# First pair's hash rows ahead of its low halves, over three queues, with the planner's numbers set anew, in a one-core LSH attention and spatial-gating kernel

## The chip, the cores and the metric

The kernel runs on one core of a Trainium2 chip. The metric is the device time of one execution in microseconds (us). The engines are called PE (TensorE, matrix products), DVE (VectorE), ACT (ScalarE), POOL (GpSimd) and SP (SyncE, which here only issues DMAs).

## The reference, cut to what matters

```python
# B, H, S, D = 4, 8, 768, 64; proj is 64 x 6
q_bits = (einsum('bhsd,dk->bhsk', q, proj) > 0)        # six hash bits per query; k_bits alike
mask = q_bucket[:, :, :, None] == k_bucket[:, :, None, :]
scores = where(mask, (q @ k.T) / sqrt(D), -1e9)
attn = softmax(scores)
x = (attn @ v), heads side by side                      # 4 x 768 x 512
h = maximum(x @ w_in, 0); u, vv = halves of h           # 512 columns each
v_n = (vv - mean) / sqrt(var + 1e-6)
v_s = einsum('ts,bsd->btd', w_spatial, v_n) + b_spatial
out = (u * v_s) @ w_out
```

## The kernel before, in words

**Tiles.** The 32 heads are taken as 16 pairs (`p` 0 to 15, four pairs to a batch element); the two heads of a pair lie in the two halves of the partitions. The 768 rows of a pair are worked in six steps (`i` 0 to 5) of 128 rows, so there are 96 score steps, written p.i here (0.0 is the very first, 5.0 the first of pair 5). f32 operands are split in a high and a low f16 half, so that a product is three products of halves.

**One step.** `scores` forms, for both heads, twelve products of halves (tile `hl`) and then four products of hash rows (tile `hk`) in the same PSUM banks: the hash rows push the scores of other buckets far down. For a head worked by queries, DVE then reduces the step to row maxima and moves it to SBUF (`low`, L525, tile `ex`), ACT or POOL forms the bias (`nb`), ACT the exponential (L535) and the f16 high half (L539, tile `pp`), DVE or POOL the low half (`rest`, L543), SP turns it with a DMA (L547, tile `pt`), and `weighted` (L653, `pv`) multiplies by v some steps later. Heads 2, 4, 6 and 8 (one in each of the pairs 1 to 4) are worked by keys: their maxima are formed ahead by `row_max` (tile `mx`), six steps of them before the pair's own first score step. The pairs after that carry only queries.

**Before a pair's first step** its q and k are loaded (`load_qk`), split (`split_qk`: one ACT copy, L412, then two DVE subtractions, L416) and hashed (`hash_rows`): a PE product (`hp`, L371), two small DVE operations (bits, L378, and scale, L382, tile `sg`), and eight DMAs (twelve from pair 5 on) that put the hash rows into `hk` (L393). For pair 0 SP and ACT issue these DMAs, four each; for all others POOL issues them.

**Weights.** Meanwhile 36 pieces of the three weight matrices come in by SP (`fetch`, L293). Those of w_in and w_out are worked by ACT and DVE with one ACT operation (`first`, L309), four DVE operations (L313, L314, L316, L318), an ACT copy (L323) and a DVE subtraction (L328); those of w_spatial only with the last two.

**MLP.** When all four pairs of a batch element are done, its gating MLP becomes filler for PE: six v units, eight u units, eight s units, six o units, cut in chunks of three products (L750) of which there are 128 to a batch element. 24 of them are v chunks and 32 are u chunks. An s unit needs the normalized v of all six v units; its low half is formed by POOL (L892, tile `vn`).

**The order** is not found on the chip. Every operation is recorded with a rank, an estimated duration and what it comes after; a planner in the kernel (`timetable`) plays the engines against these estimates, takes on a free engine the operation of the lowest rank among those that could start (or could within `LOOK`), and gives each a start. The program is then written out in the order of these starts, and on the chip each engine runs its own list strictly in that order. `LATER` shifts ranks by the name of the operation; `LAG0` is by how many steps `weighted` comes behind the scores for heads of the first batch element; the `T_` numbers say how far apart the score steps are in the plan, `begin` being the earliest start of a step. Where the planner sees PE idle for over `GAP`, it puts in small products whose result nobody reads, to keep PE busy (`warm`, L217): 444 of them.

## Time and profile before

| what | value |
|---|---|
| three timed runs | 658.12, 659.49, 662.9 us, median 659.49 |
| profiled execution, its own time | 655.07 us |
| its span in the trace | 653.3 us |
| granted PE clock | 1.00 of full speed throughout |
| busy share of the span | PE 94%, DVE 72%, ACT 73%, POOL 49% |
| instructions | 17683 |

A row of the timeline gives start, duration, engine, line, operation and tiles; "x4" means four instructions merged, and what stands in brackets is the idle time ahead of it and what ended it. An engine name with a q (SPq) is that engine's queue of DMA issues. A row of the stretches gives, after the bounds and the length, the busy time and the number of instructions of each engine. PE busy includes the `warm` products.

### The profile page before, as it was taken

What the parts mean: (1) busy time and instruction counts of PE and PEld (TensorE: products, weight loads), DVE (VectorE), ACT (ScalarE), POOL (GpSimd) and SP (SyncE); (2) the same over time, 40 slices, a digit from 0 to 9 for tenths busy, and PEclk for the clock granted to TensorE, in tenths of its full rate; (3) what the DMA queues carried; (4) which work ended last, traced back from release to release, by engine and by line L of the source; (5) the groups of instructions that cost most, each with busy time, mean ns of one, the idle gap of its engine ahead of it and who ended that gap; (6) DMA issues with size and microseconds to landing.
All of it is one profiled execution on the core that took longest, in us unless ns stands there. A gap on an engine that the chain in (4) does not pass through costs nothing.

```text
span 653.3 us, 17683 instructions
## 1 busy us (share of the span) xinstructions
PE 615.5 (94%) x7076; PEld 374.4 (57%) x7076; DVE 471.1 (72%) x986; ACT 473.7 (73%) x800; POOL 321.8 (49%) x397
## 2 busy tenths in 40 slices
PE   5789999899999999899999999998999999999997
PEld 3466767577555656455555556564555665556553
DVE  6899999898788766758879677765667587365250
ACT  3868776868898977887879887876889967463121
POOL 4565451534686859494638559376749412000000
PEclk9999999999999999999999999999999999999999
DMA  5899988997899999999998999997997989210102
GB/s 186 197 190 227 199 163 174 222 214 145 178 209 188 169 219 198 204 209 198 212 207 147 201 225 148 227 213 138 210 214 130 153 150 158 50 49 0 49 1 96
DMA packets 311682, 108.94 MB, mean 167 GB/s; under 512 B 298144, under 2 KB 301744, under 8 KB 311600
## 3 DMA queue, kind: packets, MB, share of 16 engines
q1 hardware_dynamic: 306256, 106.26, 84.4%
q0 software_dynamic: 5248, 1.52, 1.2%
q8 instruction: 55, 0.90, 0.6%
q14 instruction: 27, 0.22, 0.1%
q10 hardware_dynamic: 96, 0.04, 0.0%
HBM read 27.94 MB, written 6.29 MB: 52 GB/s over the span
## 4 chain that ended last, share of the span: by engine, by line
PE 51%; DVE 15%; DMA 11%; ACT 9%; issue 7%; POOL 5%; SPq 1%; DVEq 0%; POOLq 0%; ACTq 0%
PE sps L750 12%; PE sp L496 9%; PE ops L750 9%; PE pv L653 8%; DMA pt<-pp 6%; PE ups L750 5%; DVE ex L525 4%; PE vps L750 3%; ACT pp L539 3%; ACT ex L535 2%; POOL pp L543 2%; DVE pp L543 2%; PE vpp L750 2%; DMA hk<-sg 2%; DVE mx L600 1%
## 5 line engine op out<-in xcount | busy, mean ns | idle before, releaser
L525 DVE TENSOR_SCALAR_CACHE_REDUCE ex<-sp 128x768 f32<-128x768 f32 x168 | 155.6, 951 | 55.1 <-PE sp L496 53.0
L543 POOL TENSOR_TENSOR pp<-ex,pp 128x768 f16<-128x768 f32 x86 | 140.9, 1646 | 74.2 <-ACT pp L539 53.0
L535 ACT ACTIVATE ex<-ex,nb 128x768 f32<-128x768 f32 x168 | 155.3, 932 | 10.5 <-POOL nb L530 7.3
L539 ACT CAST pp<-ex 128x768 f16<-128x768 f32 x168 | 137.3, 826 | 4.9 <-DMA pt<-pp 3.6
L653 PEld LDWEIGHTS <-pt 128*128 128x128 f16 x3024 | 107.4, 97 | 37.3 <-DMA pt<-pp 13.3
L653 PE MATMUL pv<-vp,pt 128*128 128x65 f16 x3024 | 118.6, 193 | 7.9 <-DMA pt<-pp 7.7
L496 PE MATMUL sp<-hl 64*128 64x384 f16 x1080 | 107.4, 324 | 5.0 <-DVE ex L525 4.7
L393 POOL DMA_DIRECT2D hk<-sg x156 | 79.8, 518 | 50.8 <-issue 15.9
L543 DVE TENSOR_TENSOR pp<-ex,pp 128x768 f16<-128x768 f32 x82 | 79.7, 980 | 34.2 <-ACT pp L539 33.9
L750 PE MATMUL sps<-ws,vn 128*128 128x384 f16 x576 | 100.8, 326 | 0.1
L496 PEld LDWEIGHTS <-hl 64*128 64x128 f16 x1116 | 51.1, 94 | 56.8 <-issue 27.5
L750 PEld LDWEIGHTS <-vn 128*128 128x128 f16 x576 | 53.7, 98 | 33.5 <-issue 0.9
L750 PE MATMUL ops<-wo,g 128*128 128x512 f16 x288 | 66.1, 379 | 1.0 <-DVE sg L378 1.0
L532 ACT ACTIVATE nb<-mr 128x1 f32<-128x1 f32 x123 | 24.1, 197 | 55.9 <-DVE ex L525 55.6
L750 PE MATMUL ups<-xt,wi 128*128 128x384 f16 x348 | 62.8, 326 | 1.2 <-ACT u L919 1.2
L750 PE MATMUL vps<-wi,xt 128*128 128x512 f16 x234 | 56.9, 379 | 1.7 <-DVE sg L378 0.9
L750 PEld LDWEIGHTS <-wi 128*128 128x128 f16 x384 | 35.1, 98 | 24.1 <-issue 3.7
L750 PEld LDWEIGHTS <-g 128*128 128x128 f16 x288 | 26.7, 98 | 31.7 <-issue 1.6
L750 PEld LDWEIGHTS <-xt 128*128 128x128 f16 x288 | 25.5, 97 | 29.5 <-issue 5.4
L496 PE MATMUL sp<-hk 12*128 12x384 f16 (+2 forms) x360 | 37.1, 329 | 4.5 <-DMA hk<-mt 3.5
L940 DVE SCALAR_TENSOR_TENSOR sy<-sps,bt 128x384 f32<-128x384 f32 x32 | 17.8, 555 | 31.0 <-PE sps L750 31.0
L948 ACT CAST g<-sy 128x384 f16<-128x384 f32 x32 | 16.2, 506 | 32.3 <-DVE sy L952 28.8
(112 smaller groups left out, 786.7 us busy)
## 6 DMA issues: line engine op xcount, KB each, us to landing
qk<-kq SPq DMA_DIRECT2D x16, 768.0 KB
out<-o SPq DMA_DIRECT2D x24, 256.0 KB
v<-v SPq DMA_DIRECT2D x12, 384.0 KB
pt<-pp SPq DMA_TRANSPOSE x168
hk<-sg POOLq DMA_DIRECT2D x156, 9.0 KB, 4.0
raw<-w_in SPq DMA_DIRECT2D x8, 256.0 KB
raws<-w_in SPq DMA_DIRECT2D x8, 256.0 KB
vf<-v SPq DMA_DIRECT2D x4, 384.0 KB
```

What stands on the lines that cost most here:

```text
L393: eng.dma_start(out=hkt(p)[D * e + at:D * e + at + 2 * NB, 1 - j // 2, (j % 2) * HS:(j % 2 + 1) * HS], in_=sg[1][32 * j + 16 * e:32 * j + ...
L496: nc.tensor.matmul(ps[e][:, c - halves[0]], lhsT=src[r, l, rows], rhs=src[r, m, cs], start=(a == 0), stop=(a == len(passes) - 1))
L525: nc.vector.tensor_scalar(ex, st["sc", p, i][e], -float(2 ** 28), None, op0=ALU.max, op1=ALU.max, accum_out=st["mx", n][:, i:i + 1])
L532: nc.scalar.activation(nb, mx, AF.Copy, scale=-ISQ)
L535: nc.scalar.activation(st["e32", n, i], st["e32", n, i], AF.Exp, bias=st["nb", n][:, i:i + 1], scale=ISQ)
L539: nc.scalar.copy(st["pp", n, i][:, 0], st["e32", n, i])
L543: eng.tensor_tensor(out=st["pp", n, i][:, 1], in0=st.pop(("e32", n, i)), in1=st["pp", n, i][:, 0], op=ALU.subtract)
L600: nc.vector.reduce_max(st["mx", 2 * p + e][:, i, c:c + 1], ps[e], axis=AX.XY)
L653: nc.tensor.matmul(o, lhsT=l, rhs=m, start=(i == 0 and k == 0), stop=(i == NT - 1 and k == len(todo_) - 1))
L750: nc.tensor.matmul(c[0], lhsT=l(), rhs=r(), start=(j == 0), stop=(j == len(products) - 1))
L940: nc.vector.scalar_tensor_tensor(out=y[0], in0=c[0], scalar=1.0 / (SN * SW), in1=bt[:, hs], op0=ALU.mult, op1=ALU.add)
L948: nc.scalar.copy(gt[h][0][:, d], y[0])
```

## The change

The two small DVE operations and the eight DMAs of pair 0's hash rows get a rank ahead of everything else (`soon`), so that they go before the low halves of the same pair where they can. The eight DMAs are spread: SP issues four, ACT two, POOL two. The load of the third pair is planned behind the first score step. Beside that the planner's numbers change: `relu` later by 0.3, `LAG0` 4 for 3, `T_LAST` 5.8 for 5.95, `LOOK` 0 for 0.05, and products of the rank -9 get no added lateness.

```diff
-    LATER = {'relu': 0.1, 'first': -0.5, ...
+    LATER = {'relu': 0.4, 'first': -0.5, ...
-    def op(e, d, fn, *after, on=(), rank=4, land=0.0, dma=0.0, need=None, gives=None, alone=False):
+    def op(e, d, fn, *after, on=(), rank=4, land=0.0, dma=0.0, need=None, gives=None, alone=False, soon=False):
         later = LATER.get(fn.__name__.strip("<>"), 0.0)
-        if not isinstance(rank, tuple):
+        if soon:
+            rank = (-9, rank[1])
+        elif not isinstance(rank, tuple):
             rank = rank + later
...
-                late = (LATE_D if o.dma else LATE) if a.e == "P" and not (isinstance(a.rank, tuple) and a.rank[1] == 0) else 0.0
+                late = (LATE_D if o.dma else LATE) if a.e == "P" and not (isinstance(a.rank, tuple) and (a.rank[1] == 0 or a.rank[0] == -9)) else 0.0
...
-        t = op("V", 0.54, bits, t, on=[g0], rank=(urgent(p), 2), gives="m")
-        t = op("V", 0.24, scale, t, on=[g0, g1], rank=(urgent(p), 2), alone=True)
+        t = op("V", 0.54, bits, t, on=[g0], rank=(urgent(p), 2), gives="m", soon=p == 0)
+        t = op("V", 0.24, scale, t, on=[g0, g1], rank=(urgent(p), 2), alone=True, soon=p == 0)
...
-                q, eng = HQ_FIRST[e] if p == 0 else HQ_REST
+                q, eng = HQ_FIRST[2 * j + e] if p == 0 else HQ_REST
...
-    LAG, LAG0, LAGK = 4, 3, 2
-    T_FIRST, T_KEYS, T_QUERIES, T_THIRD, T_LAST = 5.0, 5.4, 5.55, 5.75, 5.95
+    LAG, LAG0, LAGK = 4, 4, 2
+    T_FIRST, T_KEYS, T_QUERIES, T_THIRD, T_LAST = 5.0, 5.4, 5.55, 5.75, 5.8
-    LOOK = 0.05
+    LOOK = 0
-    HQ_FIRST = (("S", nc.sync), ("A", nc.scalar))
+    HQ_FIRST = [("SAG"[k], (nc.sync, nc.scalar, nc.gpsimd)[k]) for k in (2, 0, 1, 2, 0, 1, 0, 0)]
...
             if g == 0:
                 hash_rows(1)
                 split_qk(1)
-                load_qk(2)
+                load_qk(2, now)
```

The planner's numbers move instructions on every engine over the whole program. In the changed program all line numbers behind `op` are higher by two. Three places follow.

The first is the start of DVE's list, from behind its first fills to the first two reductions of scores. Before:

```order
L416 SCALAR_TENSOR_TENSOR hl_114<-qk_108,hl_114 128x768 x2
L378 TENSOR_SCALAR sg_0_168<-hp_118,hc 128x384
L435 SCALAR_TENSOR_TENSOR vp_92<-v_0_110,vp_92 128x12x64
L382 TENSOR_SCALAR sg_0_174<-sg_0_168,hc 128x384
L416 SCALAR_TENSOR_TENSOR ws_79<-qk_112,ws_79 128x768 x2
L378 TENSOR_SCALAR sg_1_230<-hp_182,hc 128x384
L382 TENSOR_SCALAR sg_1_233<-sg_1_230,hc 128x384
L525 TENSOR_SCALAR ex_0_295,mr_293<-sp_0_0_241 128x768
L313 TENSOR_SCALAR w_291<-w_291 128x256
L525 TENSOR_SCALAR ex_0_305,mr_303<-sp_0_1_242 128x768
```

And in the changed program:

```order
L380 TENSOR_SCALAR sg_0_193<-hp_114,hc 128x384
L418 SCALAR_TENSOR_TENSOR hl_119<-qk_108,hl_119 128x768
L384 TENSOR_SCALAR sg_0_197<-sg_0_193,hc 128x384
L418 SCALAR_TENSOR_TENSOR hl_119<-qk_108,hl_119 128x768
L437 SCALAR_TENSOR_TENSOR vp_92<-v_0_110,vp_92 128x12x64
L418 SCALAR_TENSOR_TENSOR ws_79<-qk_112,ws_79 128x768 x2
L380 TENSOR_SCALAR sg_1_217<-hp_211,hc 128x384
L384 TENSOR_SCALAR sg_1_237<-sg_1_217,hc 128x384
L527 TENSOR_SCALAR ex_0_270,mr_268<-sp_0_0_219 128x768
L527 TENSOR_SCALAR ex_0_278,mr_276<-sp_0_1_220 128x768
```

Pair 0's bits now come first, its scale stands between the two low halves, and no weight operation stands between the two reductions. On ACT two of pair 0's hash DMAs now stand ahead of the split of pair 1 (tile `ws`), where four stood behind it; ACT's first weight operation, which stood ahead of the first bias, has moved behind the second exponential. On PE, 71 `warm` products stand between the hash products of pair 0 and pair 1 and none between the latter and the first scores, where it was 43 and 39. POOL issues the eight hash DMAs of pair 1 behind its two of pair 0.

The second place is DVE's list around the first step of pair 5 (`ex_0`); `w` and `wo` are weight pieces of w_out. Before:

```order
L525 TENSOR_SCALAR ex_4_2877,mr_2517<-sp_4_1_2786 128x768
L313 TENSOR_SCALAR w_2874<-w_2874 128x256
L328 SCALAR_TENSOR_TENSOR wo_104<-w_2810,wo_103 128x256
L314 TENSOR_SCALAR w_2874<-w_2874 128x256
L316 SCALAR_TENSOR_TENSOR w_2874<-raws,w_2874 128x256
L318 SCALAR_TENSOR_TENSOR w_2874<-raws,w_2874 128x256
L525 TENSOR_SCALAR ex_5_2915,mr_2517<-sp_5_1_2889 128x768
L328 SCALAR_TENSOR_TENSOR wo_104<-w_2874,wo_103 128x256
L525 TENSOR_SCALAR ex_0_2957,mr_2955<-sp_0_0_2924 128x768
L525 TENSOR_SCALAR ex_0_2964,mr_2962<-sp_0_1_2925 128x768
```

And in the changed program:

```order
L527 TENSOR_SCALAR ex_5_2864,mr_2534<-sp_5_1_2820 128x768
L316 TENSOR_SCALAR w_2840<-w_2840 128x256
L330 SCALAR_TENSOR_TENSOR wo_104<-w_2787,wo_103 128x256
L318 SCALAR_TENSOR_TENSOR w_2840<-raw_2703,w_2840 128x256
L527 TENSOR_SCALAR ex_0_2915,mr_2913<-sp_0_0_2879 128x768
L841 BN_STATS bs_0_2921<-vr_0_2902 128x6
L842 BN_AGGR mv_0_2920<-bs_0_2921 128x2
L527 TENSOR_SCALAR ex_0_2947,mr_2945<-sp_0_1_2880 128x768
L320 SCALAR_TENSOR_TENSOR w_2840<-raw_2703,w_2840 128x256
L315 TENSOR_SCALAR w_2917<-w_2917 128x256
```

The last weight operation stood just ahead of pair 5's first reduction and now four pieces of w_out are still being worked when that reduction comes. In DVE's list ahead of it there are 3 fewer of each of L313, L314 and L316, 4 fewer of L318, 4 fewer of L328 and one fewer of L543.

The third place is POOL's list around the last three low halves of the first batch element's normalized v (`vn_1`), in pairs 6 and 7; `hk_81` are pair 7's hash DMAs. Before:

```order
L892 TENSOR_TENSOR vn_1_3356<-vr_3_3345,vn_0_3355 128x512
L543 TENSOR_TENSOR pp_2_3784<-ex_2_3751,pp_2_3784 128x768
L543 TENSOR_TENSOR pp_2_3849<-ex_2_3763,pp_2_3849 128x768
L695 TENSOR_TENSOR xs_3847<-x_3776,xs_3847 128x6x64
L695 TENSOR_TENSOR xs_3847<-x_3778,xs_3847 128x6x64
L393 DMA hk_81<-sg_7_3949 12x384 x12
L892 TENSOR_TENSOR vn_1_3356<-vr_4_3443,vn_0_3355 128x512
L892 TENSOR_TENSOR vn_1_3356<-vr_5_3534,vn_0_3355 128x512
```

And in the changed program:

```order
L894 TENSOR_TENSOR vn_1_3292<-vr_3_3199,vn_0_3291 128x512
L532 TENSOR_SCALAR nb_3574<-mr_3573 128x1
L395 DMA hk_81<-sg_7_3911 12x384 x5
L545 TENSOR_TENSOR pp_3_3976<-ex_3_3918,pp_3_3976 128x768
L545 TENSOR_TENSOR pp_3_4037<-ex_3_3940,pp_3_4037 128x768
L395 DMA hk_81<-sg_7_3911 12x384 x7
L894 TENSOR_TENSOR vn_1_3292<-vr_4_3301,vn_0_3291 128x512
L545 TENSOR_TENSOR pp_5_4158<-ex_5_4132,pp_5_4158 128x768
L545 TENSOR_TENSOR pp_5_4160<-ex_5_4138,pp_5_4160 128x768
L894 TENSOR_TENSOR vn_1_3292<-vr_5_3358,vn_0_3291 128x512
```

Two low halves of scores now stand between the last two. In the plan's order the last `vn_1` stood ahead of step 7.0 and now stands behind it, while on PE the 56th chunk (the last of the v and u units) followed step 6.5 and now follows step 6.3. Over the program there are 481 `warm` products for 444: 71 for 82 ahead of step 0.0, 107 for 92 in pair 0, 141 for 163 in pairs 1 to 4, 99 for 25 in pairs 5 to 7 (89 of them between 6.4 and 7.0) and 63 for 82 after that. The MLP chunks ahead of 5.0 are 4 for 3, ahead of 6.0 they are 37 for 24, ahead of 8.0 they are 80 for 84.

More of the change, by code (lines that the diff above doesn't have):

```diff
@@ L78, in lsh_attention_spatial_gating @@
     TURN = 1.92
-    LATER = {'relu': 0.1, 'first': -0.5, 'bias': -0.3, 'bits': 0.1, 'stats': 0.3, 'half': -0.4, 'copy': 0.6, 'scale': 0.3, 'newton': -0.4, 'low': 0.6, 'exp': -0.1, 'factor': -0.3, 'turn': -0.6, 'rest': -0.1}
+    LATER = {'relu': 0.4, 'first': -0.5, 'bias': -0.3, 'bits': 0.1, 'stats': 0.3, 'half': -0.4, 'copy': 0.6, 'scale': 0.3, 'newton': -0.4, 'low': 0.6, 'exp': -0.1, 'factor': -0.3, 'turn': -0.6, 'rest': -0.1}
     ops = []
@@ L382, in scale @@
             nc.vector.tensor_scalar(sg[1], sg[0], hv[:, 1:2], None, op0=ALU.mult)
-        t = op("P", 0.8, go, at["qk", p], *after, on=[qk], rank=(urgent(p), 3), need=("m", 1))
-        t = op("V", 0.54, bits, t, on=[g0], rank=(urgent(p), 2), gives="m")
-        t = op("V", 0.24, scale, t, on=[g0, g1], rank=(urgent(p), 2), alone=True)
+        t = op("P", 0.8, go, at["qk", p], *after, on=[qk], rank=(urgent(p), 3), need=("m", 1), soon=p == 0)
+        t = op("V", 0.54, bits, t, on=[g0], rank=(urgent(p), 2), gives="m", soon=p == 0)
+        t = op("V", 0.24, scale, t, on=[g0, g1], rank=(urgent(p), 2), alone=True, soon=p == 0)
         at["hk", p] = []
@@ L395, in move @@
                         in_=sg[1][32 * j + 16 * e:32 * j + 16 * e + 2 * NB, :])
-                at["hk", p].append(op(q, 0.53 if q == "G" else 0.75, move, t, on=[g1, k], rank=(urgent(p), 3), land=2.8 if q == "G" else 1.8))
+                at["hk", p].append(op(q, 0.53 if q == "G" else 0.75, move, t, on=[g1, k], rank=(urgent(p), 3), land=2.8 if q == "G" else 1.8, soon=p == 0))
                 if four(p) and j < 2:
```

## The prediction

> **What bounds the kernel now.** I begin with the page's totals.
>
> ```profile
> PE 615.5 (94%) x7076; PEld 374.4 (57%) x7076; DVE 471.1 (72%) x986; ACT 473.7 (73%) x800; POOL 321.8 (49%) x397
> ```
>
> PE is the engine to look at, but 94% is flattered: its busy time includes the `warm` products. So I cut the span where the first scores of pairs 0, 1 and 5 start (13.2, 47.2 and 168.6 us) and at three later step starts, and ask for the busy time of each stretch, then for that of the `warm` line (L217) alone.
>
> ```profile
> 13.20:47.20 34.00, 26.59 (x386) 17.47 (x385) 27.23 (x64) 23.16 (x40) 21.43 (x27) 1.00 0.92 183
> 47.20:168.60 121.40, 112.39 (x1372) 82.19 (x1371) 113.55 (x271) 90.91 (x167) 53.62 (x70) 1.00 0.92 198
> 168.60:270.00 101.40, 95.90 (x1223) 56.07 (x1222) 75.67 (x154) 87.81 (x147) 72.74 (x83) 1.00 1.07 187
> 270.00:411.90 141.90, 140.54 (x1733) 81.13 (x1734) 106.51 (x202) 117.57 (x192) 89.31 (x109) 1.00 1.07 195
> 411.90:548.00 136.10, 131.50 (x1606) 76.21 (x1607) 94.34 (x191) 108.95 (x180) 79.60 (x93) 1.00 0.98 179
> 548.00:653.30 105.30, 100.83 (x670) 55.73 (x669) 43.56 (x91) 40.32 (x74) 1.33 (x3) 1.00 0.18 48
> ```
>
> The columns behind the length are PE, PEld, DVE, ACT, POOL, then the granted clock, the DMA share and GB/s.
>
> ```profile
> 47.20:168.60 121.40, 10.13 (x164) 9.35 (x163) 1.00 0.92 198
> 168.60:270.00 101.40, 1.56 (x25) 1.41 (x25) 1.00 1.07 187
> ...
> sum 653.30, PE 28.89 PEld 26.25; mean PE 4.13 PEld 3.75
> ```
>
> So PE does 615.5 - 28.9 = 586.6 us of real work, which the change leaves as it is. The rest, 653.3 - 586.6 = 66.7 us, is idle time or filler, and only there can the time change. Most of it lies early: nearly all of the first 13.2 us, ahead of the first scores, then 34.0 - 26.59 = 7.4 us idle in pair 0, then 9.0 idle and 10.1 of filler in pairs 1 to 4. From 168.6 us on, MLP chunks fill PE, and 15.9 us of idle time are left in 484.7 us. The early stretch is held by DVE: it is busy 113.55 of 121.40 us there, and waits little for anyone.
>
> ```profile
> DVE ex L525 <- PE sp L496: 2.4, 2, 1.8
> ```
>
> This is DVE's longest wait between 47.2 and 168.6 us: total, times, longest.
>
> **The change part by part: the head.** The first 24 us, by the timeline:
>
> ```profile
> 5.43 1.50 PE L371 MATMUL hp<-qk,hc 128*32 128x384 f32 x8 [5.43 <-DMA qk<-kq]
> 6.84 1.83 DVE L416 SCALAR_TENSOR_TENSOR hl<-qk,hl 128x768 f16<-128x768 f32 x2 [0.77 <-ACT hl L412]
> 6.87 3.24 PE L217 MATMUL warm<-ident 128*128 128x128 f16 x43
> 8.45 1.48 ACT L412 ACTIVATE ws<-qk 128x1536 f16<-128x1536 f32 x1 [0.91 <-DMA qk<-kq]
> 8.58 0.61 DVE L378 TENSOR_SCALAR sg<-hp,hc 128x384 f16<-128x384 f32 x1
> 9.97 0.32 DVE L382 TENSOR_SCALAR sg<-sg,hc 128x384 f16<-128x384 f16 x1
> 10.17 0.85 PE L371 MATMUL hp<-qk,hc 128*32 128x384 f32 x8
> 10.32 4.00 SPq L393 DMA_DIRECT2D hk<-sg  x4
> 10.32 4.00 ACTq L393 DMA_DIRECT2D hk<-sg  x4
> 13.21 4.34 POOL L393 DMA_DIRECT2D ws<-sg  x8 [8.73 <-DVE sg L382]
> 15.37 1.22 PE L496 MATMUL sp<-hk 63*128 63x384 f16 x4 [0.98 <-DMA hk<-sg]
> 16.26 0.96 DVE L525 TENSOR_SCALAR_CACHE_REDUCE ex<-sp 128x768 f32<-128x768 f32 x1 [3.35 <-PE sp L496]
> 18.27 0.43 ACT L309 ACTIVATE w<-raw 128x256 f32<-128x256 f32 x1 [8.33 <-DMA raw<-w_in]
> 18.94 0.95 DVE L525 TENSOR_SCALAR_CACHE_REDUCE ex<-sp 128x768 f32<-128x768 f32 x1
> 19.95 1.13 PE L496 MATMUL sp<-hl 64*128 64x384 f16 x11 [1.54 <-DVE ex L525]
> 23.57 0.48 PE L496 MATMUL mx<-ws 64*128 64x384 f16 x2 [0.95 <-DVE mx L600]
> ...
> DMA to landing us min/median/max: 2.1/4.2/5.5
> ```
>
> Before, scale ends at 10.29 and the hash rows let PE go on at 15.37, 5.1 us later. Now bits start when the hash products end (6.93), then one low half (1.83 / 2) and scale: 6.93 + 0.61 + 0.92 + 0.32 = 8.8. With the same 5.1 us the rows are there at 13.9. PE itself is ready about then: 71 fillers at 3.24 / 43 = 75 ns end at 6.87 + 5.35 = 12.2, the second hash products at 13.1, twelve products at 14.2, the four with the hash rows (1.22 with their wait before; 0.6 unhindered) at 14.8, against 16.6. DVE gains a little less. ACT now issues two DMAs (4.00 / 4 each) ahead of the split of pair 1: 8.8 + 2.0 + 1.48 = 12.3, DVE's two low halves to 14.1, the second bits and scale to 15.0. The first reduction starts at 15.0 for 16.26 and the second at 16.0 for 18.94, because ACT no longer waits until 18.27 for a weight piece ahead of the bias and DVE has no weight operation between the two. The second scores can start at 17.0 for 19.95: 3 us.
>
> What is late next are pair 1's eight hash rows: POOL starts them at 15.0 for 13.21, its last issue stands at 18.8, and with the median 4.2 us to landing they are there at 23.0. The first `row_max` with hash rows needs them, stood at 23.57, and step 0.2 is queued behind it on PE. That gives back most of the 3 us for PE, though exponentials and transposes of steps 0.0 and 0.1 stay ahead. I take **-2 us**, between 0 and -3.
>
> A rule speaks against the third queue. The Trainium skill, "DMA: Bandwidth & Descriptors", section "Issuing engines are not separate DMA queues", says that DMAs of all issuing engines run on the same 16 DMA engines, and that using several saves only the issue time, usually small beside the transfer. The trace half disagrees: issue took 4.00 us and the wait behind it 0.98. By the rule the head would bring 0 for -2. My sum takes nothing from the third queue either, since SP still issues four; it goes by the earlier scale.
>
> **Pairs 1 to 4.** DVE's list ahead of pair 5's first reduction is shorter by 17 weight operations and one low half of scores.
>
> ```profile
> L543 DVE TENSOR_TENSOR pp<-ex,pp 128x768 f16<-128x768 f32 x82 | 79.7, 980 | 34.2 <-ACT pp L539 33.9
> L313 DVE TENSOR_SCALAR w<-w 128x256 f32<-128x256 f32 x24 | 8.6, 363 | 1.5 <-ACT w L309 1.5
> L314 DVE TENSOR_SCALAR w<-w 128x256 uint32<-128x256 uint32 x24 | 7.3, 309 | 0.0
> L318 DVE SCALAR_TENSOR_TENSOR w<-raws,w 128x256 uint32<-128x256 uint32 x12 | 5.6, 465 | 0.0
> L328 DVE SCALAR_TENSOR_TENSOR wo<-w,wo 128x256 f16<-128x256 f32 x8 | 4.4, 554 | 0.7 <-ACT wo L323 0.7
> ```
>
> By the means, L316 taken as L318: 3 x 0.363 + 3 x 0.309 + 7 x 0.465 + 4 x 0.554 + 0.98 = 8.5 us. A stretch in which DVE is 94% busy could shorten by all of that. The other bound is PE: 112.39 us busy there, with 141 fillers for 163 (22 x 0.062 = 1.4 us less), so 111 us are its floor and -10 us the end on that side. At the other end is 0: PE also waits for hash rows and maxima that come by DMA, and in-order lists pass on half of what one engine gains. I take **-5 us**, between 0 and -10. The weight operations come later, in pair 5, where DVE has room (75.67 of 101.40 us).
>
> **Pairs 5 to 7.** Here the change spends its filler too early. By step 6.0, 37 chunks are done for 24, and all 56 chunks of the v and u units are gone after step 6.3. The next ones, of the s units, need all six normalized v, whose low halves POOL forms.
>
> ```profile
> 195.98 1.17 POOL L892 TENSOR_TENSOR vn<-vr,vn 128x512 f16<-128x512 f32 x1
> 230.34 2.28 POOL L892 TENSOR_TENSOR vn<-vr,vn 128x512 f16<-128x512 f32 x2
> 232.33 0.65 PE L750 MATMUL sps<-ws,vn 128*128 128x384 f16 x3
> ```
>
> Even before, the s units began just as the last low half ended (230.34 + 2.28 = 232.62). Now the last one stands behind step 7.0 and the chunks run out three steps earlier; the plan puts 89 fillers there. At 1.56 / 25 = 62 ns each, the 99 - 25 = 74 more fillers of these pairs cost 4.6 us of PE. I take **+4.6**. It is 0 where they stand in idle time that was there before (5.5 us in this stretch), and +9 if three steps without chunks each leave another 1.5 us open.
>
> **After that** there are 63 fillers for 82: 19 x 0.065 (28.89 / 444) = **-1.2 us**, and the idle time of 1.4, 4.6 and 4.5 us in the last three stretches may move by some 3 us either way (-4 to +3). `T_LAST` moves only starts in the plan; on the chip it changes how chunks are dealt out, and PE's work is the same.
>
> **Sum:** -2 - 5 + 4.6 - 1.2 = -3.6 us. Against the profiled execution's own 655.07 us (1.8 us beyond its span) that is 651.5. That execution is the fastest seen, 4.4 us below the median of 659.49, so against the median I forecast 659.49 - 3.6 = **656 us**.
>
> **The rivals.** *The early stretch gives all* (chance 0.20): DVE alone held pairs 1 to 4, and the fillers of pairs 6 and 7 fall into idle time. For it speaks DVE's 94%; against it, PE's 111 us floor leaves no slack. -3 - 10 + 2 - 1.2 = -12, or 647 us.
>
> *The early stretch gives nothing* (0.15): hash rows and maxima by DMA hold PE, and pair 1's late rows eat the head's gain. For it: the wait ahead of 23.57. 0 + 0 + 4.6 - 1.2 = +3.4, or 663 us, within 1%.
>
> *PE starves in pairs 6 and 7* (0.13, the slower side): the six low halves of v are POOL's, and between the first and the last of them its list now holds 24 hash DMAs, twelve low halves of scores and six of v, beside small biases: 24 x 0.51 + 12 x 1.63 + 6 x 1.17 = 39 us of work, where 36.6 us elapsed before.
>
> ```profile
> 217.48 3.25 POOL L543 TENSOR_TENSOR pp<-ex,pp 128x768 f16<-128x768 f32 x2
> 223.20 4.55 POOL L393 DMA_DIRECT2D hk<-sg  x9
> ```
>
> PE has three steps and 5.5 us of filler to bridge. If POOL's waits add more than about 12 us to the 39, PE stands still, and each us there is a us of the end. With 8 more: -1 - 0 + 13 - 1.2 = +11, or 670 us. Against it: POOL was busy 72.74 of 101.40 us in that stretch, which leaves it room to keep up.
>
> *The hash rows do not come earlier* (0.07): ACT's two issues and the landing hold the first scores, as the cited rule would have it, and the rest is as forecast: 658 us.
>
> **How the numbers follow.** The forecast has 0.45, with 651 to 661 as its own range. The range is 647 to 668: it takes in the fast rival, and leaves out the starved one and the ends, under 0.2 together. About 1% is what a measurement here can tell from no change, 652.9 to 666.1. Faster: 0.20 and the lower tail of the forecast, 0.25. Slower: 0.13 and some tail, 0.15. Within: 0.60.
>
> **What would show it.** In the changed profile the second scores at about 17 us; step 1.0 at 45 for 47.2; step 5.0 at about 161 to 162 for 168.6, with DVE's busy time ahead of it down by some 8 us; between steps 6.3 and 7.1 idle time and filler on PE of some 10 us, where the chunks now run out. Wrong it would be if step 5.0 starts no earlier, or if idle time of over 18 us lies in pairs 6 and 7.

## The result, and the profile after

The changed kernel takes 667.61 us (median of six runs, 664.9 to 670.87) against 659.35 us for the kernel before on the same chip: a ratio of 1.0125, with a 95% interval of 1.0084 to 1.0166. It is slower by about 8 us, where the prediction said 3.6 us faster. Runs that lie more than 1.5% above the fastest of their kernel are left out of every ratio here, so a ratio can differ from the quotient of the medians, and the profiles of e5 and e7 are of such runs.

The profiled execution of the changed kernel took 667.48 us, its span was 665.7. Its totals and its row of granted clock, from the page:

```profile
span 665.7 us, 17761 instructions
PE 625.2 (94%) x7113; PEld 380.9 (57%) x7113; DVE 475.8 (71%) x990; ACT 476.8 (72%) x805; POOL 322.2 (48%) x390
PEclk9799999999899999999999999999999999999999
```

The share of PE is still 94%, yet it is busy 9.7 us longer. The 7 and the 8 in the clock row are new: before, it was full throughout. Where the 12.4 us between the two spans lie is seen by stretches that begin at the same steps: the start of 1.0 (48.3 us now, 47.2 before), of 5.0 (171.3, 168.6) and of 8.0 (279.2, 270.0). The rows have the columns of the prediction's: PE, PEld, DVE, ACT, POOL, granted clock, DMA share, GB/s. First the changed kernel, all instructions and then `warm` alone:

```profile
0.00:48.30 48.30, 37.89 (x487) 26.20 (x487) 37.42 (x77) 27.95 (x41) 23.45 (x42) 0.93 0.85 182
48.30:171.30 123.00, 111.87 (x1350) 82.29 (x1350) 106.53 (x254) 90.30 (x162) 60.17 (x73) 0.99 0.92 187
171.30:279.20 107.90, 101.14 (x1282) 60.33 (x1281) 85.05 (x169) 89.87 (x155) 72.12 (x78) 0.98 1.01 181
279.20:665.70 386.50, 374.30 (x3996) 212.12 (x3995) 246.79 (x493) 268.70 (x450) 166.51 (x199) 1.00 0.82 149
...
0.00:48.30 48.30, 12.72 (x178) 11.92 (x178) 0.93 0.85 182
48.30:171.30 123.00, 9.75 (x141) 8.48 (x141) 0.99 0.92 187
171.30:279.20 107.90, 6.18 (x99) 5.58 (x99) 0.98 1.01 181
279.20:665.70 386.50, 4.17 (x63) 3.72 (x63) 1.00 0.82 149
```

And of the kernel before the two stretches that the prediction does not show:

```profile
0.00:47.20 47.20, 34.30 (x482) 23.11 (x483) 37.46 (x79) 28.14 (x44) 25.24 (x41) 1.00 0.83 192
270.00:653.30 383.30, 372.87 (x4003) 213.07 (x4002) 244.41 (x483) 266.85 (x445) 170.24 (x205) 1.00 0.79 149
...
0.00:47.20 47.20, 11.65 (x174) 10.54 (x174) 1.00 0.83 192
270.00:653.30 383.30, 5.55 (x82) 4.95 (x82) 1.00 0.79 149
```

Idle time of PE plus filler, stretch by stretch:

| stretch | before | after | difference | predicted |
|---|---|---|---|---|
| up to 1.0 | 12.90 + 11.65 = 24.6 | 10.41 + 12.72 = 23.1 | -1.4 | -2 |
| 1.0 to 5.0 | 9.0 + 10.1 = 19.1 | 11.13 + 9.75 = 20.9 | +1.7 | -5 |
| 5.0 to 8.0 | 5.5 + 1.56 = 7.1 | 6.76 + 6.18 = 12.9 | +5.9 | +4.6 |
| from 8.0 | 10.43 + 5.55 = 16.0 | 12.20 + 4.17 = 16.4 | +0.4 | -1.2 |

That sums to +6.6. The other 5.8 us are PE's own work: 625.2 - 32.8 = 592.4 for 586.6 us, with the same products. They ran slower, in three spells of half clock (6.83, 3.41 and 3.41 us long, from 25.01, 83.03 and 175.19 us on). The first stands right behind the head. The timeline of the head, the stretch of the spell, and the first `row_max` of the kernel before:

```profile
9.12 3.22 SPq L395 DMA_DIRECT2D hk<-sg  x4
15.55 0.96 DVE L527 TENSOR_SCALAR_CACHE_REDUCE ex<-sp 128x768 f32<-128x768 f32 x1
17.45 1.13 PE L498 MATMUL sp<-hl 64*128 64x384 f16 x11 [0.22 <-DVE ex L527]
...
21.35 0.33 PE L498 MATMUL mx<-ws 64*128 64x384 f16 x1
23.90 0.83 PE L498 MATMUL mx<-ws 63*128 63x384 f16 x3 [2.22 <-DMA ws<-sg]
24.43 1.85 PE L498 MATMUL sp<-hl 64*128 64x384 f16 x12
26.71 1.48 PE L498 MATMUL mx<-ws 64*128 64x384 f16 x4
```

```profile
25.00:32.00 7.00, 6.75 (x37) 3.47 (x33) 5.24 (x11) 4.94 (x8) 4.41 (x4) 0.51 0.91 114
```

```profile
22.12 0.50 PE L496 MATMUL mx<-ws 64*128 64x384 f16 x2
```

Pair 0's rows, the first reduction and the second scores are all earlier than before (10.32, 16.26 and 19.95). But then PE waits 2.22 us for pair 1's hash rows (`ws<-sg`) ahead of the first `row_max` that needs them, and soon after the granted clock is 0.51 for 7 us: twelve products of step 0.2 take 1.85 us for 1.15. Before, the two products of the last row were a plain one and, at 22.30 us in the trace, the first one with hash rows: it went without a wait, 1.6 us earlier than now, and the clock stayed full. The row at 23.57 that the prediction reads as this product is the next `row_max`, and the 0.95 us of idle time ahead of it ended with a reduction on DVE.

The profile of before (655.07 us) was a lucky execution. Every timed run lists its mean granted clock. In the 100 runs of the kernel before that stand beside these experiments, time times (1 - clock) is 3.87 us on the mean; the 68 runs with a clock of 0.994 or more have a median of 658.4 us, the other 32 of 662.5. For the changed kernel that product is 5.23 us. Taken off, 656.0 us are left before and 662.4 after. So about 6.5 of the 8 us are the order and 1.4 the clock. This split is an estimate, as a spell also moves what lies behind it.

### The profile page after: what moved, and what is told of

The parts are those of the page before. It is cut to its first block, busy times and chain, and to the rows that moved or that the text cites. A ratio compares the mean times of both kernels' runs of the same rounds, so it can differ in the third digit from the quotient of the medians.

```text
span 665.7 us, 17761 instructions
## 1 busy us (share of the span) xinstructions
PE 625.2 (94%) x7113; PEld 380.9 (57%) x7113; DVE 475.8 (71%) x990; ACT 476.8 (72%) x805; POOL 322.2 (48%) x390
## 4 chain that ended last, share of the span: by engine, by line
PE 53%; DMA 18%; DVE 12%; ACT 6%; issue 5%; POOL 4%; SPq 1%; ACTq 0%; DVEq 0%; POOLq 0%
PE sps L752 11%; DMA pt<-pp 10%; PE sp L498 10%; PE pv L655 9%; PE ops L752 8%; PE ups L752 6%; PE vps L752 4%; DVE ex L527 3%; DVE pp L545 2%; DMA hk<-sg 2%; POOL pp L545 2%; ACT ex L537 2%; PE vpp L752 1%; ACT pp L541 1%; PE mx L498 1%
## 5 line engine op out<-in xcount | busy, mean ns | idle before, releaser
L498 PE MATMUL sp<-hl 64*128 64x384 f16 x1080 | 109.7, 328 | 4.3 <-DVE ex L527 3.1
L545 DVE TENSOR_TENSOR pp<-ex,pp 128x768 f16<-128x768 f32 x84 | 85.2, 1025 | 36.2 <-ACT pp L541 36.2
L395 POOL DMA_DIRECT2D hk<-sg x158 | 83.1, 533 | 45.7 <-DVE sg L384 10.7
L752 PE MATMUL vps<-wi,xt 128*128 128x512 f16 x234 | 55.3, 380 | 1.0 <-DVE sg L380 1.0
L752 PEld LDWEIGHTS <-wi 128*128 128x128 f16 x384 | 35.2, 98 | 23.1 <-issue 2.3
L498 PE MATMUL sp<-hk 12*128 12x384 f16 (+2 forms) x360 | 38.7, 332 | 3.5 <-DMA hk<-mt 3.0
L655 PE MATMUL pv<-vf,ex 128*128 128x65 f32 x288 | 37.3, 280 | 1.7 <-ACT ex L570 1.7
```

The source lines that it names most:

```text
L395: eng.dma_start(out=hkt(p)[D * e + at:D * e + at + 2 * NB, 1 - j // 2, (j % 2) * HS:(j % 2 + 1) * HS], in_=sg[1][32 * j + 16 * e:32 * j + ...
L498: nc.tensor.matmul(ps[e][:, c - halves[0]], lhsT=src[r, l, rows], rhs=src[r, m, cs], start=(a == 0), stop=(a == len(passes) - 1))
L545: eng.tensor_tensor(out=st["pp", n, i][:, 1], in0=st.pop(("e32", n, i)), in1=st["pp", n, i][:, 0], op=ALU.subtract)
L655: nc.tensor.matmul(o, lhsT=l, rhs=m, start=(i == 0 and k == 0), stop=(i == NT - 1 and k == len(todo_) - 1))
L752: nc.tensor.matmul(c[0], lhsT=l(), rhs=r(), start=(j == 0), stop=(j == len(products) - 1))
```

## The experiments

Every kernel was timed beside the kernel before on the same chip. "Lost" means time times (1 - granted clock), mean over the runs.

### Does DVE, or PE, set the pace of pairs 1 to 4?

**e4_dve** is the kernel before without two of the four DVE operations of each weight piece, 48 in all, so the weights are not the reference's.

```diff
-  t = op("V", 0.2, lambda c=c: nc.vector.tensor_scalar(c["w"], ...
-  t = op("V", 0.2, lambda c=c: nc.vector.tensor_scalar(c["wu"], ...
+  t = op("V", 0.2, lambda c=c: None, ...       # twice
```

> The kernel before without two of the DVE operations on every weight piece of w_in and w_out (lines 313 and 314, 48 operations, some 16 us of DVE, 44 of them ahead of step 5.0), so the weights are wrong; the order of everything else is the same. Theory of the prediction (DVE sets the pace of pairs 1 to 4): step 5.0 comes 8 to 14 us earlier and the end 5 to 12 us. Rival (pairs 1 to 4 are held by chains of waits through PE, ACT and DMA, in which DVE's work stands beside): step 5.0 moves by less than 4 us.

Measured: 660.58 us, 0.9997 (0.9955 to 1.0038). The stretch from 1.0 to 5.0:

```profile
49.20:171.90 122.70, 114.71 (x1373) 83.67 (x1371) 106.04 (x229) 90.36 (x166) 53.99 (x69) 0.97 0.89 194
```

DVE's busy time falls from 113.55 to 106.04 us, and the stretch goes from 121.40 to 122.70. (The 40 operations that are missing in it lasted 13.6 us by their means; the rows of DVE overlap, so its busy time falls by 7.5 us only.) A spell of half clock, 6.83 us long, costs 3.4 of these; without it at most 2 of DVE's 7.5 us came through, and none in the time. Step 5.0 came at 171.9 us for 168.6. DVE alone does not set the pace there.

**e7_pe** is the kernel before without one of the four product passes in the score steps of pairs 1 to 4 (about 9 us of PE); the scores lose that part.

```diff
-  sums(ps, p, slice(i * P, (i + 1) * P), ALL, False)
+  sums(ps, p, slice(i * P, (i + 1) * P), ALL[:2] + ALL[3:] if 0 < p < 5 else ALL, False)
```

> The kernel before with one of the four passes of products left out in the score steps of pairs 1 to 4 (four of the sixteen products of 24 steps, about 9 us of PE; the scores there lose a correction); same order. It is the counterpart on PE of the run that took 15 us of DVE's work out of the same pairs and moved nothing. Theory A (PE sets the pace there): step 5.0 comes 5 to 9 us earlier. Theory B (a chain of waits across engines and DMAs, in which a score step's products are one link): 0 to 4 us.

Measured: 670.72 us, 1.0135 (1.0053 to 1.0217); 13.9 us lost (12.3 in the three runs of the ratio). Step 5.0 came at 178.5 us for 168.6.

```profile
124.00:172.00 48.00, 45.76 (x449) 35.26 (x449) 37.71 (x88) 29.53 (x52) 17.14 (x26) 0.75 0.90 190
```

PE, given less to do, is granted 0.75 of its clock over 48 us: the saved products come back as slow ones in this execution.

**e5_nofill14** and **e10_half14** are the kernel before without the 163 fillers of pairs 1 to 4, and with half of them.

```diff
+  if at["S", 1, 0].start <= t < at["S", 5, 0].start:
+      continue                    # e10: n = n // 2
```

> The kernel before without the 163 fillers of pairs 1 to 4 (10.1 us of PE there); everything else in the same order. Theory A (PE, with its fillers in the way, sets the pace of pairs 1 to 4, as 112.4 us busy of 121.4 would have it): step 5.0 comes 4 to 10 us earlier and the time falls by as much, apart from half clock. Theory B (the fillers stand in time in which PE waits anyway, and they hold the clock): step 5.0 moves by less than 2 us once half clock is counted, more spells of half clock, and the time is the same or up to 6 us longer.

> Before with half of the fillers of pairs 1 to 4 (about 81 of 163). Without any the kernel gained some 5 us of order and lost some 10 us more to the half clock. If the two trade evenly along the way: 659 to 662 us. If half of the fillers are enough to keep the clock: 655 to 658 us, with a granted clock of 0.99 or more in most runs. If the clock needs all of them: 662 to 666 us.

Measured: 663.59 us for e5, 1.0015 (0.9974 to 1.0057), 13.3 us lost (10.6 in the six runs of the ratio); 666.59 us for e10, 1.0119 (1.0067 to 1.0171), 6.8 us lost. In e5 one spell is nearly 24 us long:

```profile
114.60:138.50 23.90, 23.63 (x125) 14.76 (x127) 13.83 (x31) 13.33 (x24) 9.93 (x11) 0.50 0.66 159
```

The fillers pay for themselves by the clock. Without any, what is left after the lost time is 651.1 us, with half 660.9, with all 656.0: no even trade, so the "5 us of order" that e10's expectation took from e5 was too neat a reading, and e10 came out above all three of its forecasts.

The stretch from 1.0 to 5.0 in the kernel before and in these four, one trace each; half the length of its spells is an estimate of what they cost:

| kernel | taken out there | stretch | half of its spells | without it |
|---|---|---|---|---|
| before | nothing | 121.4 | none | 121.4 |
| e4 | 7.5 us of DVE | 122.7 | 3.4 | 119.3 |
| e7 | 96 products, about 9 us of PE | 129.9 | 11.9 | 117.9 |
| e5 | all fillers, 10.1 us of PE | 133.3 | 17.1 | 116.2 |
| e10 | half the fillers, about 5 us of PE | 124.6 | 3.4 | 121.2 |

By this estimate at most about half of what was taken off one engine would come through, and the clock takes more than that back in e5 and e7; their runs in the ratio, too, lose 8.1 and 9.8 us more than the kernel before on that chip (2.5). The list of PE's waits in the stretch (total, times, longest) shows what stands there beside DVE, in the changed kernel and then before:

```profile
PE sp L498 <- ACT ex L570: 3.3, 7, 1.3
PE pv L655 <- ACT ex L570: 1.7, 4, 0.8
```

```profile
PE sp L496 <- ACT ex L568: 1.0, 2, 0.9
```

PE's longest item in the changed kernel is ACT's exponential of the heads by keys, 5.0 us for 1.0. No run took work off ACT, so that rival stands untested.

### Are the fillers of pairs 6 and 7 waste, or cover for a wait?

**e6_nofill57** is the changed kernel without the 99 fillers of pairs 5 to 7 (the same edit, between steps 5.0 and 8.0).

> The changed kernel without its 99 fillers of pairs 5 to 7 (6.2 us of PE); everything else in the same order. If the fillers themselves are the 4.6 us that the prediction put on pairs 5 to 7, steps 7.0 and 8.0 come 5 us earlier and the time falls to about 662. If PE really waits there for want of chunks, idle time takes their place, steps 7.0 and 8.0 stay within 2 us apart from half clock, and the time is 666 to 671.

Measured: 671.28 us, 1.014 (1.0055 to 1.0226); 9.2 us lost. Steps 6.3 to 7.0 in the changed kernel, and then in this one, where the columns are again those of the stretches; the last row is this kernel's list of waits there (total, times, longest):

```profile
227.00:247.40 20.40, 17.92 (x290) 13.21 (x289) 14.91 (x25) 17.54 (x31) 14.66 (x19) 1.00 1.10 210
```

```profile
225.35:246.17 20.82, 13.52 (x200) 8.87 (x200) 14.90 (x25) 18.68 (x32) 14.61 (x19) 0.93 1.03 210
```

```profile
PE pv L657 <- DMA pt<-pp: 4.7, 1, 4.7
```

The stretch is as long without them, and PE is busy 4.4 us less: the fillers lay in a real gap. PE there waits for turned exponentials (`pt`), with no chunk left to do meanwhile. Why there is none, the changed kernel's trace shows: its last u chunks, the last but one and the last low half of v, and its first s chunk are

```profile
233.46 1.14 PE L752 MATMUL ups<-xt,wi 128*128 128x384 f16 x6
244.85 1.56 POOL L894 TENSOR_TENSOR vn<-vr,vn 128x512 f16<-128x512 f32 x1
250.81 1.15 POOL L894 TENSOR_TENSOR vn<-vr,vn 128x512 f16<-128x512 f32 x1
251.27 0.65 PE L752 MATMUL sps<-ws,vn 128*128 128x384 f16 x3
```

For 16.7 us PE has no chunk, until POOL comes to the last low half; before, the s units began at 232.33 without such a gap. That is the prediction's step on pairs 5 to 7, and it holds. Taking the fillers away only adds a spell of 6.83 us.

### Is it the head, or the numbers?

**e2_head** is the kernel before with everything on the head and no number changed; **e3_ranks** is the kernel before with the four numbers only.

```diff
+  soon=p == 0 ..., HQ_FIRST over three queues, load_qk(2, now)      # e2
```

```diff
+  'relu': 0.4, LAG0 = 4, T_LAST = 5.8, LOOK = 0                      # e3
```

> Only the head of the change (hash rows of pair 0 first and over three queues, third pair's load behind the first scores); relu, LAG0, T_LAST and LOOK as before. Theory (the head's gain is undone by the clock and by DVE weight work that is put off): steps 0.0 to 0.1 as early as in the changed kernel (second scores at 17 us), the same wait for pair 1's hash rows, half clock behind it, and a time of 661 to 667, slower than before. Rival (the numbers of the planner do the harm): 655 to 659, not slower than before.

> Only the planner's numbers (relu, LAG0, T_LAST, LOOK) as in the changed kernel; the head as before. Theory (the head and what the clock makes of it do the harm): no spell of half clock in the first 50 us, 656 to 662, the same as before within 0.5%. Rival (the numbers do the harm, by a starved PE in pairs 5 to 7 and chunks left for the end): 664 or more, with idle time and fillers of 10 us or more in pairs 5 to 7.

Measured: 684.98 us for e2, 1.0391 (1.0314 to 1.0468), and 683.11 us for e3, 1.0377 (1.0298 to 1.0456). Each half alone is far worse than both together, above both forecasts of e2 and above the theory's of e3 (its rival, 664 or more, came by the number). They lose it at different places: at step 1.0 e3 is 8.9 us behind the kernel before and e2 0.4, at 8.0 it is 10.4 and 20.5, at the end 26.5 and 34.2. So the planner answers either edit with an order that differs over the whole program, and the numbers belong to one such order.

**e8_nolag**, **e11_tlast** and **e12_look** are the changed kernel with one number put back each.

```diff
-  LAG0 = 4 / T_LAST = 5.8 / LOOK = 0
+  LAG0 = 3 / T_LAST = 5.95 / LOOK = 0.05
```

> The changed kernel with LAG0 set back to 3. Head alone took 685, the numbers alone 683, both together 667.6 and neither 659. Theory (the head needs LAG0 = 4: with the weighted products one step later the first batch element's PE waits for turned scores vanish): 678 to 690, like the head alone. Rival (LAG0 matters little, another of the numbers carries it): 664 to 671.

> The changed kernel with T_LAST back at 5.95, all else as changed. Theory (numbers of the planner are tuned to one order; any turn of one of them gives another order that costs 1 to 4 per cent or, rarely, gains): 670 to 690 us. Rival (T_LAST 5.8 deals the chunks worse, as the fillers of pairs 6 and 7 and the tail suggest): 657 to 663 us, with pairs 5 to 7 as in the changed kernel and the tail shorter.

> The changed kernel with LOOK back at 0.05, all else as changed. Theory (any number turned by itself gives another order): 670 to 690 us. Rival (LOOK 0 is what let the weight operations slip behind pair 5 and the chunks run out early): 655 to 662 us, with fewer than 30 fillers between steps 6.3 and 7.0 and step 8.0 at 270 to 274.

Measured: 695.15 us, 1.0518 (1.0442 to 1.0594); 671.12 us, 1.0175 (1.0128 to 1.0222); 688.5 us, 1.042 (1.0359 to 1.0481). Put back, `LAG0` and `LOOK` make the changed kernel slower still; `T_LAST` alone cannot be told from it (1.0175 against 1.0125, with intervals that overlap). `relu` was not put back by itself. So none of these three numbers carries the loss, and with them the re-planned order is still worse than the old one.

### Can filler buy the clock back?

**e1_clock** is the changed kernel with 82 more small products in PE's list, where the clock had dropped: 36 ahead of the first `row_max`, 38 ahead of step 2.0, 8 ahead of 5.0.

```diff
+  HOLD = {(2, 0): 38, (5, 0): 8}
+  for _ in range(fill):
+      nc.tensor.matmul(spare, lhsT=ident, rhs=ident, start=True, stop=True)
```

> The changed kernel with 82 more fillers at three places where its PE stands idle just ahead of a spell of half clock: 36 ahead of the first row_max (2.2 us idle there), 38 ahead of the plain products of step 2.0 (1.96 us idle), 8 ahead of those of step 5.0. Nothing else differs. Theory (the clock): PE's real work grew by 5.8 us because three spells of half clock (13.65 us together, half of it lost) follow these idle times; the spells vanish, PE's real work falls back to about 587 us, and the time falls by 4 to 6 us, to about 662. Rival (order alone): the spells cost nothing that the end sees, or the fillers cost what they save: the time stays at 667 within 1.5 us.

Measured: 676.22 us, 1.0267 (1.0196 to 1.0338). The profile has four spells at other places, 17.1 us together, and 9.1 us are lost over the runs, more than without these fillers (5.23). Neither forecast came: the spells did not vanish but moved, and 8.6 us were added. So the run does not test what spells cost; that they were the whole loss is contradicted by those 5.23 us, only 1.4 more than the kernel before loses.

### The head alone, on the old order

**e9_handmoved** keeps the old plan and moves only the head's instructions behind the planner's back; PE's list is that of before, word for word.

```diff
+  z = max(low half's start, hash product's start + 0.01)
+  bits_.start, at["hl", 0][1].start, scale_.start = z - 0.001, z, z + 0.001
+  for k, o in enumerate(at["hk", 0]):
+      o.start = z + 0.002 + 0.0001 * k                   # POOL 2, SP 4, ACT 2
+  at["qk", 2].start = 0.001 + first weight piece's start
```

> The planner's order of before is kept on every engine, and only the head's instructions are moved by hand: pair 0's bits ahead of the low halves, scale between them, its eight hash DMAs on POOL, SP and ACT right behind scale, the third pair's load behind the first weight piece. PE's list, fillers included, is that of before. Theory (the head is worth what the prediction's first step gave it, and the loss comes from the order planned anew): second scores 2 to 3 us earlier, step 1.0 at 45 to 46.5 for 47.2, and where the half clock takes no more than before, 656 to 659 us, 1 to 3 below before. Rival 1 (the start of PE shifted against the rest of the order sets off the half clock, whatever the order behind it): spells of 10 us or more in the trace, 664 to 672 us. Rival 2 (PE makes up for a late start before pair 5 anyway, because its own work is the pace): step 5.0 within 1 us of before, 659 to 661 us.

Measured: 662.84 us (12 runs), 1.0044 (1.001 to 1.0078); 6.8 us lost. Taken off, 656.1 us are left, as for the kernel before (656.0). So, by this estimate, the head change by itself was worth nothing by its order and cost clock; the time falls between the forecasts. PE's timeline up to the first `row_max` with hash rows, and the stretches about it:

```profile
18.52 1.13 PE L498 MATMUL sp<-hl 64*128 64x384 f16 x11 [1.11 <-DVE ex L527]
...
20.69 0.33 PE L498 MATMUL mx<-ws 64*128 64x384 f16 x1
23.81 0.47 PE L498 MATMUL mx<-ws 63*128 63x384 f16 x1 [2.78 <-DMA ws<-sg]
```

```profile
20.00:23.30 3.30, 1.03 (x9) 0.16 (x9) 2.69 (x6) 3.23 (x6) 1.14 (x3) 1.00 1.02 318
23.30:33.50 10.20, 8.80 (x53) 4.56 (x55) 6.80 (x15) 8.17 (x14) 5.30 (x5) 0.50 0.76 115
```

The second scores came at 18.5 us for 19.95, but that `row_max` at 23.81 for 22.30. The rows of pair 1 are what is late. A part of the reason shows in the list of DMA issues between 8 and 27 us (times issued, KB each, median us from issue to landing), before and then in the changed kernel, with POOL's issue of these rows there:

```profile
ws<-sg POOLq DMA_DIRECT2D x8, 9.0 KB, 4.2
```

```profile
ws<-sg POOLq DMA_DIRECT2D x8, 9.0 KB, 5.8
...
15.78 4.09 POOL L395 DMA_DIRECT2D ws<-sg  x8 [5.11 <-DVE sg L384]
```

POOL needs as long to issue them (4.09 us for 4.34), but it begins at 15.78 for 13.21, because the second scale comes later on DVE, and they take 1.6 us longer to land. Five more runs looked for the reason. **e13_rows_hand** is e9 with pair 1's rows shared by POOL and SP, **e14_rows_after** and **e15_rows_before** are the changed kernel and the kernel before with the same sharing.

```diff
   q, eng = HQ_FIRST[2 * j + e] if p == 0 else HQ_REST
+  if p == 1 and e == 0:
+      eng = nc.sync
```

> The hand-moved head on the order of before, and beside it pair 1's eight hash rows shared by POOL and SP, four each, SP's behind its load of v. Theory (pair 1's late rows take the head's gain back: PE waits 2.8 us for them ahead of the first row_max with hash rows and is then granted half its clock): the last row is issued at 18 for 20.3 us, that row_max starts 1.5 to 2.5 us earlier than 23.8, no or shorter half clock behind it, step 1.0 at 45 to 48 for 50.4, and 655 to 659 us. Rival (rows land no earlier, because the large loads on the DMA engines hold them, or the half clock comes all the same): row_max at 23 to 24, 661 to 665 us.

> The changed kernel with the same sharing of pair 1's hash rows. Theory: first row_max with hash rows 1.5 to 2.5 us earlier than 23.9, the 6.8 us of half clock behind it gone, step 1.0 at 45 to 46.5 for 48.3; the loss of the order behind it stays, so 662 to 665 us. Rival (the rows are held by the DMA engines, not by POOL's issue): 666 to 669 us with row_max at 23.5 to 24.5.

> Before with only pair 1's hash rows shared by POOL and SP. There SP is busy with pair 0's rows and two weight loads until about 17.5 us, so its four rows go out no earlier than POOL's last did (17.55). Theory (the rows matter only where the first scores come early): no change, 657 to 661 us. Rival (the sharing by itself helps, by less crowded POOL): 653 to 656 us.

Measured: 660.27 us, 1.0017 (0.9986 to 1.0049); 665.77 us, 1.0106 (1.0064 to 1.0148); 658.6 us, 0.9988 (0.9953 to 1.0023). The `row_max` in e14, with the stretch from 1.0 to 5.0, and in e13:

```profile
21.18 1.11 PE L501 MATMUL mx<-ws 64*128 64x384 f16 x4
...
45.10:171.40 126.30, 113.35 (x1352) 82.80 (x1352) 105.53 (x254) 90.63 (x163) 59.15 (x73) 0.97 0.91 184
```

```profile
23.42 0.48 PE L500 MATMUL mx<-ws 63*128 63x384 f16 x1 [1.93 <-DMA ws<-sg]
```

In e14 the wait is gone, there is no spell behind it, and step 1.0 starts at 45.1 for 48.3 us. But 5.0 starts at 171.4 for 171.3: pairs 1 to 4 take 126.3 us for 123.0 (half of that difference is a second spell), and the gain is gone. In e13 a wait of 1.93 us and a spell of 6.83 us remained, so there issue time was not all. Why the same sharing takes the wait away in e14 and not in e13, with the third pair's load issued alike (13.07 and 13.23 us), was not found.

**e16_rows_hand2** is e13 with the second weight piece fetched behind SP's four rows.

```diff
+  second = at["piece", 1]
+  second[0].start = at["hk", 1][6].start + 0.001
```

> As the hand-moved head with shared rows, but the second weight piece is fetched behind SP's four hash rows instead of ahead of them, as in the changed order, where the wait was gone; the piece's ACT and DVE work goes behind the second exponential's half and the second step's reductions. Theory (the rows were held in the queue behind that fetch and the two large loads): the first row_max with hash rows goes at 21 to 22 for 23.4 us, no half clock behind it, step 1.0 at 44.5 to 46 for 47.2 before; and 655 to 658 us against 658 to 660 for before. Rival (the rows are late for another reason, or PE's other waits bring the half clock there): row_max after 23 us, 659 to 663 us.

Measured: 659.97 us, 0.9997 (0.9964 to 1.0031). The wait was hardly shorter, with a spell of 3.41 us behind it, so that piece was not the reason:

```profile
22.87 0.32 PE L502 MATMUL mx<-ws 63*128 63x384 f16 x1 [1.78 <-DMA ws<-sg]
```

**e17_load_first** is e13 with the third pair's load issued some 2 us earlier: SP takes two of pair 0's rows for four, and then at once that load.

```diff
-  enumerate((2, 0, 1, 2, 0, 1, 0, 0))      # POOL 2, SP 4, ACT 2
+  enumerate((2, 0, 1, 2, 0, 1, 2, 2))      # POOL 4, SP 2, ACT 2
-  at["qk", 2].start = 0.001 + first weight piece's start
+  at["qk", 2].start = at["hk", 0][7].start + 0.0001
```

> As the hand-moved head with pair 1's rows shared (the 1.93 us wait), but the third pair's load goes out about 2 us earlier: SP issues two of pair 0's hash rows for four (POOL four, ACT two) and then at once that load. Theory (pair 1's rows land late because that load, moved behind pair 0's rows, is on the DMA engines just then: to landing 5.5 to 5.8 us in the kernels with the earlier head, 4.2 in before): landing of POOL's rows back at 4.2 to 4.8 us, the first row_max with hash rows at 21 to 22.3 for 23.4, the wait ahead of it under 1 us and no half clock behind it, step 1.0 at 45.5 to 47, 655 to 658 us. Rival (the load is not what holds them): landing at 5.3 us or more, row_max after 23 us, 659 to 662 us.

Measured: 657.01 us (12 runs), 0.9972 (0.9946 to 0.9997); 3.2 us lost. Its rows of the same views:

```profile
ws<-sg POOLq DMA_DIRECT2D x4, 9.0 KB, 4.5
```

```profile
10.99 0.36 SPq L341 DMA_DIRECT2D qk<-kq  x1
21.77 0.32 PE L500 MATMUL mx<-ws 63*128 63x384 f16 x1 [0.92 <-DMA ws<-sg]
```

```profile
20.00:34.00 14.00, 10.65 (x114) 5.58 (x107) 12.45 (x27) 13.49 (x23) 9.38 (x8) 1.00 0.98 210
46.20:168.50 122.30, 113.97 (x1375) 82.87 (x1375) 112.26 (x271) 90.83 (x166) 55.98 (x69) 0.99 0.90 196
```

The load goes out at 10.99 us (13.36 in e9), the rows land in 4.5 us, the wait is 0.92, no spell follows and step 1.0 starts at 46.2 for 47.2. The load that the change moved behind pair 0's rows was on the DMA engines when pair 1's rows came: in e9 it was issued at 13.36 us and had landed at 18.91, and POOL issued the rows from 16.04 on. Of this last edit the load and the loads queued behind it come earlier together, so they are shown as a group. This is the fastest version of those tried, 0.3% below the kernel before; its interval just leaves out no change, and it is the best of several, so the gain is not sure.

## Why the prediction was wrong, point by point

**The head (-2 predicted, -1.4 measured).** The mechanism came as written: rows issued from 9.12 us, the first reduction at 15.55 for 16.26, the second scores at 17.45 for 19.95. The prediction named pair 1's rows as what is late next, but it held the row at 23.57 for the product that needs them. That product stood at 22.30 before, so rows at 23.0 would have been late already by its own sum. And it priced them by POOL's issue and the old 4.2 us: it missed that the moved load shares the engines with them (5.8 us), and that half clock can follow a longer wait there. The -1.4 leaves out what that half clock cost; by the start of step 1.0 the changed kernel is 1.1 us behind. The cited section of the Trainium skill, "DMA: Bandwidth & Descriptors", "Issuing engines are not separate DMA queues", says that all issuers share 16 engines. The trace agrees on that half of the rule: sharing the issue (e13) left a wait of 1.93 us, an earlier load (e17) 0.92. On the changed order, though, sharing alone took the wait from 2.22 to 0.13 us (e14), so issue time was not small there. Step 1.0 at 45 was promised; it came at 48.3 and, with the wait gone, at 45.1 (e14).

**Pairs 1 to 4 (-5 predicted, +1.7 measured) is the step that failed.** DVE's list did get shorter, by 113.55 - 106.53 = 7.0 us for the 8.5 worked out, and the stretch got 1.6 us longer, about half the length of its one spell of 3.41 us: nothing of the 7.0 came through, and step 5.0 came no earlier (171.3 for 168.6), which the prediction had named as the sign of being wrong. I had read 94% busy, with few waits, as the bound. But an engine whose in-order list is planned to fit the others can be as busy as the plan makes it without setting the pace. e4 took 7.5 us from DVE alone and gained nothing; e7 took products from PE and lost. Where step 1.0 came 3.2 us earlier (e14, against the changed kernel) or 1.0 us (e17, against before), 5.0 came no earlier (171.4 for 171.3, 168.5 for 168.6), though a spell of 3.41 us, some 1.7 us, has a part in each. What holds that stretch stays open: the runs exclude DVE's work as the sole holder, where PE's work was trimmed the clock answered, and ACT, for which PE waits more than before, was not tried.

**Pairs 5 to 7 (+4.6 predicted, +5.9 measured)** came as argued: the chunks run out after 6.3, the fillers cost 4.6 us more (6.18 - 1.56) and 1.3 us more idle time stands beside them. The starved rival's condition came: from the first to the last low half of v 53.5 us elapsed (198.46 to 251.96), 14.5 above its 39 of work, where it asked for 12. Its price did not: the stretch lost 5.9 us, not 13. e6 shows that what PE's list stands before meanwhile are the turned exponentials; that no chunk bridges the wait is due to POOL's late low halves, as argued.

**After that (-1.2 predicted, +0.4 measured):** fewer fillers, as counted, and as much more idle time, inside the bounds given.

**PE's work "which the change leaves as it is"** was the second false step. The products are the same, their time is not: +5.8 us in the profiled execution, about 1.4 in the mean of the runs. The sum had no term for the clock, because the one profile of before showed none lost. The errors by stretch are 0.6 + 6.7 + 1.3 + 1.6 = 10.2 us. With the 5.8 they make up the distance from -3.6 to the +12.4 of the profiled executions, and with the mean 1.4 that from 656.0 to 667.6.

**Among the rivals** the one that gave nothing early (663 us) came nearest in its terms; it lacked the clock, 1.3 us of pairs 5 to 7 and what pairs 1 to 4 lost. The starved one (670 us) is nearer by the number, by luck, as its 13 us did not come. That the measured time lies inside the range, by 0.4 us, is no merit of the sum either: its upper end was set to leave the starved rival out.

## What to carry to other kernels

A busy share tells how full a list is, not that it sets the pace: before a shorter list is priced as a gain, ask which wait behind it ends last, or take work off that engine alone and time it. When a transfer is moved out of the way of one small DMA, look for the next small DMA that it then meets, and price its landing at the busier time. Where an order is planned as a whole, an edit is worth what the new order is worth; move the few instructions by hand on the old order first, as the two can differ by more than the edit.

## What the runs showed of the hardware

The half clock came in spells of 3.41, 6.83, 10.24 us and up to 23.9, and idle time far shorter than a spell could precede one. At the first `row_max` with hash rows, one profile each:

| kernel | PE's wait ahead of it | half clock that begins within 2 us of it |
|---|---|---|
| before | none | none |
| e14 | 0.13 | none |
| e17 | 0.92 | none |
| e12 | 0.98 | none |
| e8 | 1.53 | none |
| e16 | 1.78 | 3.41 |
| e2 | 1.81 | none |
| e13 | 1.93 | 6.83 |
| e6 | 1.98 | 6.83 |
| after | 2.22 | 6.83 |
| e11 | 2.68 | none |
| e9 | 2.78 | 10.24 |

The Trainium skill, "TensorE: Matmul & The Clock Gate", section "What's actually happening", puts the window in which PE's activity is judged at about 3.4 us, with half and full speed alone; the lengths and the granted values agree. Its section "HAM oscillation — how this bites in real kernels" warns of gaps above 3.4 us. Here waits of 1.78 to 2.78 us, with the shorter gaps around them, could be enough: in e9 PE was busy 1.03 of the 3.30 us up to the spell. The table is no rule, though: e2 and e11 had such a wait and no spell at once (they, e8 and e12 have one of 3.41 us that begins 5 to 6 us behind it), and e4, e7 and e3, in whose code the head is that of before, each show 3.41 us of half clock between 19 and 34 us with no wait ahead of this product.

In each trace all spells begin on one grid of 3.413 us: in the changed kernel those at 25.01, 83.03 and 175.19 us lie 17 and 27 steps apart. Whether a wait brings a spell may then depend on where it falls in that grid, and executions of one kernel may differ by it; no run here settles that. In the 100 runs of before, a us of lost clock went with 0.8 us of time (correlation 0.76).
